# First weights as four tiles by half the rows, and block 1's layernorm root and scale moved into block 0's output stage

## The chip, the cores and the metric

The program runs on one core of one Trainium2 chip. The metric is the device time of one execution in microseconds (us), as a median over runs. A profiled execution also has a span, from its first to its last instruction; the span is about 1.4 us shorter than the time of the same run.

The engines are PE (TensorE, matmuls), PEld (its weight loads), DVE (VectorE), ACT (ScalarE), POOL (GpSimd) and SP (SyncE, which only issues DMAs here).

## The reference

Two layers read the same layernormed input of 2048 rows by 1024 features, in bf16, and their outputs are added to it.

```python
xn = layernorm(x)                                # 2048 x 1024, eps 1e-5
# A: diagonal state space layer, 1024 complex states
Bu = xn @ B_bar.T                                # complex
h[t] = Lam_bar * h[t-1] + Bu[t]                  # sequential over 2048 rows
yA = 2 * real(h @ C.T) + xn * Dskip
# B: dense, mish, dense, F = 3584
hB = xn @ w1 + b1
yB = (hB * tanh(softplus(hB))) @ w2
out = x + yA + yB
```

## The kernel before

The rows are worked in NB = 4 blocks of 512. A block has three stages on PE:

1. First product: `xn @ w1`, 28 tiles f of 128 columns, 8 matmuls each. DVE adds the bias and empties the PSUM bank into `hb`, ACT makes the mish in four groups of seven tiles.
2. Projection: `xn @ B`, 8 steps j with two PSUM banks each. DVE multiplies both banks with a table (`mt`), which turns the complex scan into a real one.
3. Output stage: `act @ w2` and `h @ C` into all 8 banks, while DVE does the scans.

Weights go through a ring of seven slots of 512 KB. Each helper call records one instruction with the buffers it reads and writes; semaphore waits follow from these. The order of calls is the order on each engine.

```python
    def ring_load():                                  # next weight item into its slot
        ...
        if kind == "w1":                              # all 1024 rows, 256 columns: runs of 512 B
            dst = ring[:, s, :].rearrange("p (k f) -> p k f", k=NK)
            src = B_w1[:, g * 256:(g + 1) * 256].rearrange("(k p) f -> p k f", p=P)
        else: ...                                     # w2
        SP.dma(lambda e: e.dma_start(dst, src), s_ring[s], writes=[b_ring[s]])
```

Block 1's layernorm is done during block 0. The statistics come at tiles 14 to 20, and then, all on DVE, the reciprocal root (15 small operations, a bit trick with three Newton steps) and four scalings:

```python
    def ln_rsqrt():
        ...                                           # v + eps, shift, subtract from the magic number
        for _ in range(3):                            # four operations a step
            ...
    def ln_scale(blk, q):
        vop(lambda e: e.tensor_scalar(xn[:, q, :], xx[:, i, q, :], mv[:, q, 0:1], rv[1][:, q:q + 1],
                                      op0=ALU.subtract, op1=ALU.mult), ...)

    def project_in(blk):
        for j in range(NJ):
            bank = banks_of(j)                        # 2 * ((j + 2) % 4)
            ...                                       # 16 matmuls into banks bank, bank + 1
            for s in range(2):                        # the table multiply: reads both banks
                vop(lambda e, ...: e.tensor_tensor(mt[:, s, :, :], u, tab..., op=ALU.mult), ...)
            ...                                       # an add and a subtract into hT

        def side(f):                                  # block 0: extra work after tile f
            if f == 13: ...                           # tables on ACT
            if f in (7, 8, 9, 10):
                coefficients(f - 7)
            if f in (9, 11, 12, 13):
                ln_skip(0, (9, 11, 12, 13).index(f))  # x += xn * Dskip
            if f in (14, 16, 18, 20):
                ln_stats_only(1, (f - 14) // 2)
            if f == 22:
                ln_rsqrt()
            if f in (23, 24, 25, 26):
                ln_scale(1, f - 23)
            ...                                       # transposes of B and C

        for f in range(NF):
            first_tile(blk, f)
            side(f)
        project_in(blk)
        ...
        for j in range(NJ):
            recur(blk, j)                             # scan of step j
            if blk == 0 and j == 0:
                mish_mul(3)
            if blk == 0:
                scale_C(j)
        ...
        tail(blk)                                     # output stage
```

## Time and profile before

| | before |
|---|---|
| time, median of 6 runs | 622.90 us (622.65 to 624.14) |
| span of the profiled run | 622.1 us |
| PE's share of the chain that ended last | 97% |
| PE's waits after its warm-up | 0.51 us for a weight load, 0.94 us for DVE |
| output stage of block 0 / of block 1, in the chain | 77.09 / 75.97 us |

A busy share does not bound a kernel; the chain does. PE has 97% of the chain, and one 512-column matmul costs 48.35 us / 224 = 215.9 ns in every block. The list of waits shows whom PE waited for, with the total, the number of times and the longest:

```profile
PE ps L465 <- POOL kon L333: 1.4, 1, 1.4
PE ps L727 <- DVE mt L674: 0.9, 1, 0.9
PE ps L504 <- DMA ring<-in_B_w_dram: 0.5, 1, 0.5
```

The first is the start of a warm-up. The other two are all that can be won by waiting less. The chain in order of time (start, length, what) shows where the second lies:

```profile
19.74 39.71 PE ps L649 x184
59.45 27.63 PE ps L669 x128
87.08 4.12 PE ps L727 x19
91.20 0.03 issue
91.22 2.37 DVE mt L674 x2
93.59 0.04 issue
93.63 70.54 PE ps L727 x326
164.17 48.35 PE ps L649 x224
```

At 87.08 us PE begins the output stage of block 0. Its 27th matmul needs bank 2, which DVE's last table multiply, from 91.22 us, has yet to read.

Why is DVE late? Its timeline (start, length, engine, line, operation, tiles, shapes, count; a bracket at the end is idle time before it) in the stretch before:

```profile
57.48 1.41 DVE L656 TENSOR_SCALAR hb<-ps,par 128x512 bf16<-128x512 f32 x2
58.81 0.16 DVE L415 TENSOR_SCALAR rv<-mv 128x4 f32<-128x4 f32 x1
...
63.05 0.16 DVE L425 TENSOR_TENSOR rv<-rv 128x4 f32<-128x4 f32 x1
63.13 0.74 DVE L656 TENSOR_SCALAR hb<-ps,par 128x512 bf16<-128x512 f32 x1
63.79 0.54 DVE L429 TENSOR_SCALAR xn<-xx,mv,rv 128x1024 bf16<-128x1024 bf16 x1
...
67.59 0.75 DVE L656 TENSOR_SCALAR hb<-ps,par 128x512 bf16<-128x512 f32 x1
68.25 2.35 DVE L674 TENSOR_TENSOR mt<-ps,tab 128x1024 bf16<-128x1024 f32 x2
70.64 0.42 DVE L677 TENSOR_TENSOR hT<-mt 128x512 bf16<-128x512 bf16 x1
70.98 0.41 DVE L679 TENSOR_TENSOR hT<-mt 128x512 bf16<-128x512 bf16 x1
71.53 2.35 DVE L674 TENSOR_TENSOR mt<-ps,tab 128x1024 bf16<-128x1024 f32 x2
```

There is no bracket: DVE never idles. The root (L415 to L425) and the scalings (L429) stand ahead of the table multiplies, the first of which starts at 68.25 us, although PE had finished its banks at about 59.45 + 27.63 / 8 = 62.9 us. One step takes DVE 71.53 - 68.25 = 3.28 us and PE 27.63 / 8 = 3.45 us, so eight steps win back only 1.4 us of the 5.35 us.

### The profile page before, as it was taken

How to read it: one execution, taken by the hardware profiler on the slowest of the kernel's cores; microseconds unless marked ns; L12 is line 12 of the kernel's file. 1: busy time of each engine (PE TensorE's matmuls, PEld its weight loads, DVE VectorE, ACT ScalarE, POOL GpSimd, SP SyncE). 2: the span in 40 equal slices, each digit the busy share in tenths (PEclk: the TensorE clock that was granted, in tenths of full speed). 3: DMA queues.
4: the chain of work that ended last, by engine and by line, in shares of the span. 5: the costliest groups of instructions: out<-in, count | busy, mean ns of one | idle time of the engine just before them, and what ended most of it. 6: DMA issues, size and time to landing. Idle time of an engine off the chain costs nothing.

```text
span 622.1 us, 7394 instructions
## 1 busy us (share of the span) xinstructions
PE 617.1 (99%) x2961; PEld 287.8 (46%) x2961; DVE 467.2 (75%) x690; ACT 244.6 (39%) x158; POOL 50.9 (8%) x47
## 2 busy tenths in 40 slices
PE   8999999999999999999999999999999999999998
PEld 7544444444444444444444444444444444444444
DVE  6799999999557599999047759999624856999603
ACT  5679996332069950000008992000000999000000
POOL 1999000000100000000010000000000000000000
DMA  8999996750265400784064430285304542033001
GB/s 246 246 245 263 236 170 190 187 165 0 101 209 164 135 2 9 232 172 129 14 189 143 162 101 1 71 223 158 90 35 135 151 154 67 1 117 120 1 0 68
DMA packets 124477, 79.41 MB, mean 128 GB/s; under 512 B 48923, under 2 KB 106907, under 8 KB 124443
## 3 DMA queue, kind: packets, MB, share of 16 engines
q1 hardware_dynamic: 120944, 71.64, 43.5%
q10 hardware_dynamic: 2538, 4.14, 1.8%
q0 software_dynamic: 960, 3.15, 1.7%
q8 instruction: 24, 0.39, 0.3%
q14 instruction: 11, 0.08, 0.0%
HBM read 63.19 MB, written 4.19 MB: 108 GB/s over the span
## 4 chain that ended last, share of the span: by engine, by line
PE 97%; DMA 1%; DVE 0%; SPq 0%; issue 0%
PE ps L727 48%; PE ps L649 30%; PE ps L669 18%; DMA ring<-in_B_w_dram 1%; PE ps L504 1%; DVE mt L674 0%; SPq L287 0%; PE ps L741 0%; PE ps L386 0%; SPq L291 0%; SPq L318 0%; DVE xx L795 0%
## 5 line engine op out<-in xcount | busy, mean ns | idle before, releaser
L727 PE MATMUL ps<-ring,act 128*128 128x512 bf16 x896 | 194.2, 379 | 0.9 <-DVE mt L674 0.9
L649 PE MATMUL ps<-xnT,ring 128*128 128x512 bf16 x856 | 185.4, 379 | 0.0
L627 ACT ACTIVATE act<-hb 128x3584 bf16<-128x3584 bf16 x16 | 50.9, 3183 | 246.3 <-DVE hb L656 246.0
L727 PEld LDWEIGHTS ps<-ring,act 128*128 128x128 bf16 x896 | 87.6, 98 | 106.9 <-DVE mt L674 1.4
L649 PEld LDWEIGHTS ps<-xnT,ring 128*128 128x128 bf16 x856 | 83.7, 98 | 100.8
L656 DVE TENSOR_SCALAR hb<-ps,par 128x512 bf16<-128x512 f32 x112 | 82.8, 747 | 56.5 <-PE ps L649 55.3
L669 PE MATMUL ps<-xnT,BT 128*128 128x512 bf16 x512 | 111.2, 379 | 0.0
L727 PE MATMUL ps<-CT,hT 128*128 128x512 bf16 x506 | 109.9, 379 | 0.0
L674 DVE TENSOR_TENSOR mt<-ps,tab 128x1024 bf16<-128x1024 f32 x64 | 75.3, 1219 | 13.3 <-PE ps L669 11.8
L669 PEld LDWEIGHTS ps<-xnT,BT 128*128 128x128 bf16 x512 | 50.1, 98 | 60.4
L727 PEld LDWEIGHTS ps<-CT,hT 128*128 128x128 bf16 x506 | 49.5, 98 | 59.7
L692 DVE TENSOR_TENSOR_SCAN hT<-cs,qi,hT 128x512 bf16<-128x512 f32 x48 | 58.9, 1267 | 0.0
L772 DVE TENSOR_TENSOR xx<-ps,xx 128x1024 bf16<-128x1024 f32 (+1 forms) x16 | 18.8, 1189 | 45.5 <-PE ps L727 45.4
L629 ACT ACTIVATE act<-act 128x3584 bf16<-128x3584 bf16 x16 | 51.0, 3190 | 0.2
L628 ACT ACTIVATE act<-act 128x3584 bf16<-128x3584 bf16 x16 | 51.0, 3190 | 0.2
L697 DVE TENSOR_TENSOR mt<-hT,tab 128x1024 bf16<-128x1024 bf16 x64 | 41.4, 688 | 1.1
L634 DVE TENSOR_TENSOR act<-act,hb 128x3584 bf16<-128x3584 bf16 x16 | 32.5, 2034 | 1.3 <-ACT act L629 1.3
L287 POOL DMA_DIRECT2D xx<-in_A_x_dram x12 | 6.7, 560 | 254.0 <-DVE xx L772 146.4
L603 ACT ACTIVATE ct<-CT,cs 128x512 f32<-128x512 bf16 x16 | 11.5, 718 | 28.8 <-DVE CT L605 24.5
L628 ACT ACT_TABLE_LOAD x16 | 20.5, 1283 | 0.3
L629 ACT ACT_TABLE_LOAD x16 | 20.5, 1283 | 0.3
L692 DVE TENSOR_TENSOR_SCAN hT<-cs,hT 128x512 bf16<-128x512 f32 x16 | 18.7, 1208 | 0.0
(82 smaller groups left out, 280.1 us busy)
## 6 DMA issues: line engine op xcount, KB each, us to landing
ring<-in_B_w_dram SPq DMA_DIRECT2D x112, 512.0 KB, 3.9
out_dram<-xx ACTq DMA_DIRECT2D x15, 256.0 KB, 2.1
xx<-in_A_x_dram POOLq DMA_DIRECT2D x12, 256.0 KB, 5.6
xx<-in_A_x_dram SPq DMA_DIRECT2D x3, 256.0 KB, 6.3
xx<-in_A_x_dram SPq DMA_DIRECT2D x2, 128.0 KB, 2.2
dsk<-in_A_Dskip_dram SPq DMA_DIRECT2D x1, 256.0 KB, 5.5
xnT<-xn SPq DMA_TRANSPOSE x12, 4.5
BT<-in_A_B_re_dram SPq DMA_TRANSPOSE x8, 5.7
```

Of the source, the lines that this page charges most:

```text
L627: aop(lambda e: e.activation(a, hs, AF.Exp), reads=[b_hb[g % 2]], writes=[b_act[g]])
L628: aop(lambda e: e.activation(a, a, AF.Ln, bias=1.0), reads=[b_act[g]], writes=[b_act[g]])
L629: aop(lambda e: e.activation(a, a, AF.Tanh), reads=[b_act[g]], writes=[b_act[g]])
L634: vop(lambda e: e.tensor_tensor(a, a, hs, op=ALU.mult), reads=[b_act[g], b_hb[g % 2]], writes=[b_act[g]])
L649: PE.mm(lambda e, k=k: e.matmul(ps[:, bank, :], lhsT=wt[:, k, fi * P:(fi + 1) * P], rhs=xnT[:, k, :], start=k == 0, stop=k == NK - 1), rea ...
L656: vop(lambda e: e.tensor_scalar(hb[:, hs, :], ps[:, bank, :], b1(f), None, op0=ALU.add), reads=[b_ps[bank], b_par], writes=[b_hbf[hs]])
L669: PE.mm(lambda e, j=j, ci=ci, k=k, bank=bank: e.matmul(ps[:, bank + ci, :], lhsT=BT[:, ci, j, k, :], rhs=xnT[:, k, :], start=k == 0, stop= ...
L674: vop(lambda e, s=s, u=u, j=j: e.tensor_tensor(mt[:, s, :, :], u, tab[:, s, j, :].unsqueeze(1).to_broadcast([P, 2, TB]), op=ALU.mult), rea ...
L692: vop(lambda e, ci=ci, init=init: e.tensor_tensor_scan(out=hT[:, ci, j, :], data0=cj("r", j).to_broadcast([P, TB]), data1=hT[:, ci, j, :], ...
L697: vop(lambda e, s=s: e.tensor_tensor(mt[:, s, :, :], hT[:, :, j, :], tab[:, s, j, :].unsqueeze(1).to_broadcast([P, 2, TB]), op=ALU.mult), ...
L727: PE.mm(lambda e: e.matmul(ps[:, u, :], lhsT=lhsT, rhs=rhs, start=st_, stop=last), reads=reads, writes=[b_ps[u]], first=st_, last=last)
L772: vop(lambda e: e.tensor_tensor(xr, src, xr, op=ALU.add), reads=b_ps[bank:bank + n] + [b_x], writes=[b_x])
```

## The change

It has three parts. *Weights:* the `w1` items become tiles of 512 rows by 512 columns, four of which hold the first eight tiles f; the contiguous runs are 1 KB instead of 512 B, the first tiles' matmuls are ordered to use the first load fully before the second, and slots are released in pairs. *Root and scale:* block 1's reciprocal root becomes one Sqrt on ACT and one reciprocal on DVE, and it and the four scalings move behind the first scan of the output stage; the transposes that use them come two tiles later. *Skip:* coefficients and skip stand one or two tiles sooner. The intent is to have weights sooner at the start and DVE on time for the projection.

```diff
         if kind == "w1":
-            dst = ring[:, s, :].rearrange("p (k f) -> p k f", k=NK)
-            src = B_w1[:, g * 256:(g + 1) * 256].rearrange("(k p) f -> p k f", p=P)
+            dst = ring[:, s, :].rearrange("p (k f) -> p k f", k=NK // 2)
+            r0 = (g % 2) * D // 2
+            src = B_w1[r0:r0 + D // 2, (g // 2) * 512:(g // 2 + 1) * 512].rearrange("(k p) f -> p k f", p=P)
...
+    def ln_root():
+        y = rv[1][:, :]
+        aop(lambda e: e.activation(y, mv[:, :, 1], AF.Sqrt, bias=kon[:, 2:3]), reads=b_mv + [b_kon], writes=[b_rv[1]])
+        vop(lambda e: e.reciprocal(y, y), reads=[b_rv[1]], writes=[b_rv[1]])
...
-    for f in range(NSPLIT):
+    for f in range(4):
         first_half(f, 0, 0, NK // 2)
-        if f == 3:
-            first_transpose(2)
-            first_copy(2, VE)
+    for f in range(4):
         first_half(f, 0, NK // 2, NK)
-        if f == 3:
-            first_transpose(3)
-            first_copy(3, VE)
+        if f in (1, 3):
+            q = 2 + f // 2
+            first_transpose(q)
+            first_copy(q, VE)
+    for f in range(4, NSPLIT):
+        first_half(f, 0)
...
-        if fi == 1:
+        if f % 4 == 3:
+            item_done()
             item_done()
...
-            if blk + 1 < NB and f in (7, 9, 11, 13):
-                transpose_dma((f - 7) // 2)
+            if blk + 1 < NB and f in (9, 11, 13, 15):
+                transpose_dma((f - 9) // 2)
...
-            if f in (7, 8, 9, 10):
-                coefficients(f - 7)
-            if f in (9, 11, 12, 13):
-                ln_skip(0, (9, 11, 12, 13).index(f))
+            if f in (5, 6, 7, 8):
+                coefficients(f - 5)
+            if f in (8, 9, 11, 12):
+                ln_skip(0, (8, 9, 11, 12).index(f))
             if f in (14, 16, 18, 20):
                 ln_stats_only(1, (f - 14) // 2)
-            if f == 22:
-                ln_rsqrt()
-            if f in (23, 24, 25, 26):
-                ln_scale(1, f - 23)
...
             if blk == 0 and j == 0:
                 mish_mul(3)
+                ln_root()
+                for q in range(NQ):
+                    ln_scale(1, q)
```

Cut: the indexing of the new tiles in the matmuls.

More of the change, by code (lines that the diff above doesn't have):

```diff
@@ L497, in build_kernel, with w1_tile @@
     NSPLIT = 5
+    def w1_tile(base, f, k):
+        s = (base + 2 * (f // 4) + k // (NK // 2)) % NRING
+        wt = ring[:, s, :].rearrange("p (k f) -> p k f", k=NK // 2)
+        return s, wt[:, k % (NK // 2), (f % 4) * P:(f % 4 + 1) * P]
     def first_half(f, half, k0=0, k1=NK):
-        s, fi = f // 2, f % 2
-        wt = ring[:, s, :].rearrange("p (k f) -> p k f", k=NK)
         ts = slice(half * 256, half * 256 + 256)
         for k in range(k0, k1):
-            PE.mm(lambda e, k=k: e.matmul(ps[:, f, ts], lhsT=wt[:, k, fi * P:(fi + 1) * P], rhs=xnT[:, k, ts],
-                                          start=k == 0, stop=k == NK - 1),
+            s, w = w1_tile(0, f, k)
+            PE.mm(lambda e, k=k, w=w: e.matmul(ps[:, f, ts], lhsT=w, rhs=xnT[:, k, ts],
+                                               start=k == 0, stop=k == NK - 1),
                   reads=[b_ring[s]] + [b.parts[k // 4] for b in b_xnT[2 * half:2 * half + 2]], writes=[b_ps[f]],
                   first=half == 0 and k == 0, last=half == 1 and k == NK - 1)
-    for f in range(NSPLIT):
+    for f in range(4):
         first_half(f, 0, 0, NK // 2)
-        if f == 3:
-            first_transpose(2)
-            first_copy(2, VE)
+    for f in range(4):
         first_half(f, 0, NK // 2, NK)
-        if f == 3:
-            first_transpose(3)
-            first_copy(3, VE)
+        if f in (1, 3):
[4 more added lines that the diff above has]
+        first_half(f, 0)
     aop(lambda e: e.activation(c("dt"), ldt, AF.Exp), reads=[b_par], writes=[b_cs["dt"]])
@@ L642, in first_tile @@
     def first_tile(blk, f):
-        s = n_item[0] % NRING
-        fi, bank, hs = f % 2, f % 8, f % (2 * GF)
-        wt = ring[:, s, :].rearrange("p (k f) -> p k f", k=NK)
+        bank, hs = f % 8, f % (2 * GF)
         if blk == 0 and f < NSPLIT:
@@ L648, in first_tile @@
         for k in range(0 if blk == 0 and f < NSPLIT else NK):
-            PE.mm(lambda e, k=k: e.matmul(ps[:, bank, :], lhsT=wt[:, k, fi * P:(fi + 1) * P], rhs=xnT[:, k, :],
-                                          start=k == 0, stop=k == NK - 1),
+            s, w = w1_tile(n_item[0], f % 4, k)
+            PE.mm(lambda e, k=k, w=w: e.matmul(ps[:, bank, :], lhsT=w, rhs=xnT[:, k, :],
+                                               start=k == 0, stop=k == NK - 1),
                   reads=[b_ring[s]] + b_xnT, writes=[b_ps[bank]], first=k == 0, last=k == NK - 1)
-        if fi == 1:
+        if f % 4 == 3:
+            item_done()
             item_done()
```

## The prediction

> **What bounds the kernel.** TensorE: the chain of waits gives PE 97% of the 622.1 us span. A 512-column matmul costs 215.9 ns (chain: 48.35 us for 224) in every stage, at granted clock 1.00, so only idle PE time can be won. The list of PE's waits has two holes after the warm-up: 0.51 us at 11.09 us, where the third tile of the first product waits for the second weight load (issued 3.78, landed 11.55 by the trace's DMA records); and 0.94 us at 92.69 us, where block 0's output stage needs a PSUM bank that VectorE has not read (releaser: mt, the table multiply).
>
> **What the change does.**
>
> 1. Weight loads. Same bytes and count, but contiguous runs of 1 KB instead of 512 B. In the DMA records the early 512 B packets took 28–32 ns, the 2 KB ones about 95; interpolated, an estimate of 50–55 ns for 1 KB, 10% less than two halves. (The Trainium skill, "DMA: Bandwidth & Descriptors", section "Why small descriptors are slow", gives a fixed overhead per packet; these times agree in direction.) Loads landed 1.6 us apart; I expect 1.45–1.5, so the second lands near 11.1 us. The first load still feeds 16 matmuls, so the 0.51 us hole shrinks to 0–0.2. Tile 4 now needs load 3 (landed 14.81 before) at about 14.4 us: a hole up to 0.3 us is possible. Net gain 0.3 us (0 to 0.5).
>
> 2. VectorE before block 0's projection. In the timeline the reciprocal root took 58.81 to 63.13 us and the four scalings 0.46 us each beyond the evictions: 6.2 us. VectorE began the table multiplies at 68.25 us although the first banks were complete at about 62.9, and recovers only 0.17 us a step (3.28 against PE's 3.45). Without the 6.2 us it reaches them on time and ends near 89.5 us, 3 us before PE needs the bank. The 0.94 us hole vanishes.
>
> 3. The work put back: one Sqrt on ScalarE, one reciprocal, four scalings after the first scan. ScalarE pays one more table switch, 1.28 us in this trace (the figure of the skill's "ScalarE: Activation LUTs", section "What ACT_TABLE_LOAD costs"), inside idle gaps of 4.3 us. VectorE finished that stage at 157.2 us with slack to 160.6, and starts it 4 us earlier: no cost. Later transposes of block 1 still end long before use. Coefficients and skip sooner fill VectorE's idle gaps at 20–29 us: no effect on PE.
>
> 4. Ring slots are released in pairs. Only load 13 is doubtful: it queues behind another pair of B transposes, lands at an estimated 50.5–52 us instead of 48.65, and is needed at 52.7. Probably no hole; about 1 us at worst.
>
> **Sum.** 0.94 + 0.3 = 1.25 us off the critical path, of the 6.2 us that VectorE sheds. Prediction 621.5 us against 622.8, range 620.5 to 623.0. Chances: faster by over 2% 0.5%, within 2% 99%, slower by over 2% 0.5%.
>
> **What would show it.** No wait of PE for DVE mt near 92 us; PE's wait for ring at 11 us at most 0.2 us; VectorE's first table multiply at about 63 us, thereafter waiting for PE; 1 KB packets in place of 512 B; one or two more ScalarE table loads; PE enters the 512-column matmuls at 19.3–19.5 us instead of 19.7.
>
> **What would make it wrong.** A new PE wait for ring at tile 4 (about 14.4 us) or near 52 us (load 13) that eats the gain; 1 KB packets not faster; run-to-run spread (1.5 us among the three runs before) as large as the gain.

## More of the kernel before

In the experiments the profiled run is one of the timed runs.

Block 1's x is loaded by the POOL queue, between two groups of GpSimd work that compute phases for the tables (`if j == 3: load_x(PO, 1, q)`).

## The result

| | before | after |
|---|---|---|
| time, median of 6 runs | 622.90 us (622.65 to 624.14) | 621.84 us (621.43 to 622.33) |
| span of the profiled run | 622.1 us | 620.9 us |
| PE enters the 512-column matmuls, in the chain | 19.74 us | 19.64 us |
| output stage of block 0, in the chain | 77.09 us | 75.97 us |
| last table multiply of block 0 ends | 93.58 us | 89.38 us |

The ratio of the fast runs is 0.998, with a 95% interval of 0.9967 to 0.9993. A ratio here is the mean time of one kernel's fast runs over that of the other's of the same rounds, so it is not quite the ratio of the medians. The gain of about 1.06 us is small but clear of the spread.

In the changed kernel the lines have other numbers: L661 is the first product, L682 the projection, L740 the output stage, L687 the table multiply, L388 the transposes of the first x tiles, L516 the first product's split tiles. PE's waits:

```profile
PE ps L472 <- POOL kon L335: 1.4, 1, 1.4
PE ps L388 <- DVE xn L376: 0.6, 1, 0.6
```

Both old waits are gone; a new one of 0.6 us stands in the start, at 7.86 us (see below). The chain over the same stretch has no DVE piece:

```profile
19.64 39.71 PE ps L661 x184
59.36 27.63 PE ps L682 x128
86.99 75.97 PE ps L740 x352
162.96 48.35 PE ps L661 x224
```

And DVE's timeline ahead of the projection:

```profile
53.76 3.38 DVE L669 TENSOR_SCALAR hb<-ps,par 128x512 bf16<-128x512 f32 x5
57.67 0.75 DVE L669 TENSOR_SCALAR hb<-ps,par 128x512 bf16<-128x512 f32 x1 [0.52 <-PE ps L661]
59.40 0.75 DVE L669 TENSOR_SCALAR hb<-ps,par 128x512 bf16<-128x512 f32 x1 [0.97 <-PE ps L661]
62.85 2.36 DVE L687 TENSOR_TENSOR mt<-ps,tab 128x1024 bf16<-128x1024 f32 x2 [2.70 <-PE ps L682]
...
66.30 2.36 DVE L687 TENSOR_TENSOR mt<-ps,tab 128x1024 bf16<-128x1024 f32 x2 [0.30 <-PE ps L682]
```

Now DVE waits for PE: 2.70 us before the first table multiply, and 0.30 us before each later one. Of the 1.2 us between the two profiled spans, 77.09 - 75.97 = 1.12 us come from the output stage and 19.74 - 19.64 = 0.1 us from the start.

### The profile page after: what moved, and what is told of

It reads as the page before. It is cut to its first block, busy times and chain, and to the rows that moved or that the text cites. A ratio compares the mean times of both kernels' runs of the same rounds, so it can differ in the third digit from the quotient of the medians.

```text
span 620.9 us, 7382 instructions
## 1 busy us (share of the span) xinstructions
PE 616.8 (99%) x2961; PEld 287.4 (46%) x2961; DVE 462.3 (74%) x676; ACT 247.9 (40%) x161; POOL 50.7 (8%) x47
## 4 chain that ended last, share of the span: by engine, by line
PE 98%; DVE 1%; DMA 1%; SPq 0%; issue 0%
PE ps L740 49%; PE ps L661 30%; PE ps L682 18%; PE ps L516 1%; DMA xx<-in_A_x_dram 1%; DVE stats L348 0%; PE ps L754 0%; DVE xn L376 0%; PE ps L388 0%; SPq L291 0%; DVE xnT L401 0%; DVE xx L808 0%; DVE mv L353 0%; DVE par L495 0%; DVE rs L372 0%
## 5 line engine op out<-in xcount | busy, mean ns | idle before, releaser
L740 PE MATMUL ps<-ring,act 128*128 128x512 bf16 x896 | 194.0, 379 | 0.0
L661 PE MATMUL ps<-xnT,ring 128*128 128x512 bf16 x856 | 185.4, 379 | 0.0
L740 PEld LDWEIGHTS ps<-ring,act 128*128 128x128 bf16 x896 | 87.7, 98 | 105.7
L661 PEld LDWEIGHTS ps<-xnT,ring 128*128 128x128 bf16 x856 | 83.7, 98 | 100.8
L682 PE MATMUL ps<-xnT,BT 128*128 128x512 bf16 x512 | 111.2, 379 | 0.0
L740 PE MATMUL ps<-CT,hT 128*128 128x512 bf16 x506 | 109.9, 379 | 0.0
L687 DVE TENSOR_TENSOR mt<-ps,tab 128x1024 bf16<-128x1024 f32 x64 | 75.4, 1220 | 17.2 <-PE ps L682 16.6
L682 PEld LDWEIGHTS ps<-xnT,BT 128*128 128x128 bf16 x512 | 50.1, 98 | 60.4
L740 PEld LDWEIGHTS ps<-CT,hT 128*128 128x128 bf16 x506 | 49.5, 98 | 59.7
```

The source lines that it names most:

```text
L661: PE.mm(lambda e, k=k, w=w: e.matmul(ps[:, bank, :], lhsT=w, rhs=xnT[:, k, :], start=k == 0, stop=k == NK - 1), reads=[b_ring[s]] + b_xnT, ...
L682: PE.mm(lambda e, j=j, ci=ci, k=k, bank=bank: e.matmul(ps[:, bank + ci, :], lhsT=BT[:, ci, j, k, :], rhs=xnT[:, k, :], start=k == 0, stop= ...
L687: vop(lambda e, s=s, u=u, j=j: e.tensor_tensor(mt[:, s, :, :], u, tab[:, s, j, :].unsqueeze(1).to_broadcast([P, 2, TB]), op=ALU.mult), rea ...
L740: PE.mm(lambda e: e.matmul(ps[:, u, :], lhsT=lhsT, rhs=rhs, start=st_, stop=last), reads=reads, writes=[b_ps[u]], first=st_, last=last)
```

## The experiments

The three parts can be taken alone, as they touch separate lines. All kernels gave a correct result. Each had five timed runs (half_packets six), beside runs of the kernel before on the same chip; no single gain of 1 us is 2%, so all verdicts are "same" and the intervals and the traces decide.

| kernel | weights | root and scale | skip | runs, us | ratio (95% interval) | PE waits for mt |
|---|---|---|---|---|---|---|
| ln_only | old | moved | old | 621.51 to 621.97 | 0.9981 (0.9968 to 0.9993) | none |
| skip_only | old | old | sooner | 621.95, 622.00, 622.93, 623.06, 623.07 | 0.9994 (0.9982 to 1.0007) | none in the profile |
| weights_only | new | old | old | 622.43 to 623.13 | 0.9998 (0.9984 to 1.0011) | 0.9 us |
| after_again | new | moved | sooner | 621.50 to 622.52 | 0.9985 (0.9972 to 0.9997) | none |
| undo_ln | new | old | sooner | 621.53 to 622.47 | 0.9977 (0.9965 to 0.9990) | none |
| no_weights | old | moved | sooner | 621.41 to 622.41 | 0.9980 (0.9968 to 0.9992) | none |

New weights with the moved root and scale and the old skip were not run.

### ln_only: the root and scale alone

The edit is the hunks with `ln_root`, the removed `ln_rsqrt` and `ln_scale` lines and the later transposes, on the kernel before.

> The kernel before with only the layernorm root and scale moved into the output stage. Theory (VectorE's backlog before the projection of block 0 is what makes PE wait at 92.7 us, and the root and scale are that backlog): PE's wait for DVE mt disappears, VectorE's first table multiply starts at 62.9 to 63.5 us instead of 68.25, the block 0 output stage takes 75.97 us in the chain instead of 77.09; span 621.0 us, 1.1 below the 622.1 before, time ratio 0.998. Rival A (the weight loads give the gain): no change, 622.1. Rival B (the sooner coefficients and skip are needed): the wait stays in part.

Measured: 621.79 us median, ratio 0.9981. The first table multiply starts at 62.37 us, and PE has no wait left but its warm-up. This part alone gives the whole gain, so rivals A and B fall as far as they say that another part is needed. PE's waits:

```profile
PE ps L470 <- POOL kon L333: 1.4, 1, 1.4
```

### skip_only and skip_again: the coefficients and skip alone

```diff
-            if f in (7, 8, 9, 10):
-                coefficients(f - 7)
-            if f in (9, 11, 12, 13):
-                ln_skip(0, (9, 11, 12, 13).index(f))
+            if f in (5, 6, 7, 8):
+                coefficients(f - 5)
+            if f in (8, 9, 11, 12):
+                ln_skip(0, (8, 9, 11, 12).index(f))
```

> The kernel before with only the coefficients and the skip sooner. The theory as predicted says that they give PE nothing: span 622.1 and the 0.94 us wait stays. But in the changed kernel VectorE evicted tile 13 at 38.1 us instead of 39.9, so rival B says that this alone puts VectorE about 1.8 us ahead, which is more than the 0.94 us that PE waits: first table multiply near 66.4 us, last one ends near 91.8 us, and the wait disappears too, span 621.0. Then the two parts are each sufficient and their gains do not add.

Measured: the profile shows what rival B said (first table multiply at 66.48 us, the last ends at 91.81 us, no wait of PE for mt, span 620.6 us), but three of five times were 622.93 to 623.07 us, as slow as the kernel before, and two near 622. In this profile DVE has a wait that the kernel before has not (DVE's waits from 20 to 62 us):

```profile
DVE hb L656 <- PE ps L649: 1.6, 2, 1.0
DVE stats L408 <- DMA xx<-in_A_x_dram: 0.7, 1, 0.7
```

DVE now comes so early to the statistics of block 1 that its x has not landed. That gave theory C: the landing of block 1's x decides what the sooner skip is worth. The kernel was run again for its scatter:

> skip_only once more, for its scatter. Theory C (the landing of block 1's x tile decides): times again either near 622.0 or near 623.0; if the profile falls on a slow one, VectorE's wait for x before the statistics is longer than 0.8 us, the last table multiply ends after PE wants the bank, and PE waits for mt. In skip_only the margin was 0.3 to 0.5 us (last multiply ended at 91.81, PE used the bank from 92.2).

Measured: 621.55, 621.89, 622.11, 622.14 and 624.12 us (ratio 0.9981, interval 0.9968 to 0.9994); the profile fell on the 624.12. In it, over the same 20 to 62 us, DVE's waits are

```profile
DVE stats L408 <- DMA xx<-in_A_x_dram: 5.3, 2, 3.8
DVE hb L656 <- PE ps L649: 1.6, 2, 1.0
```

and PE's, over the whole span, are

```profile
PE ps L465 <- POOL kon L333: 1.4, 1, 1.4
PE ps L727 <- DVE mt L674: 1.2, 1, 1.2
PE ps L669 <- DVE hb L656: 0.8, 1, 0.8
PE ps L386 <- DVE xn L374: 0.4, 1, 0.4
```

The four x loads, issued from 35.6 us on, landed at 42.1, 48.9, 49.7 and 50.2 us, against 42.0 to 45.5 in skip_only. DVE lost 5.3 us at the statistics and the hole came back, with a second one at the projection. Theory C holds on the trace of a slow run and the trace of a fast run of the same kernel. No profile fell on one of skip_only's runs near 623 us, so for these it is inferred.

### skip_x_early and skip_x_late: x sooner and later

skip_only with the POOL queue's x loads in another place:

```diff
     for j in range(NJ):
         phases(j)
-        if j == 3:
+        if j == 1:        # skip_x_early;  j == 4 in skip_x_late
             for q in range(NQ):
                 load_x(PO, 1, q)
```

> skip_only with block 1's x loads issued two phase groups earlier on the pool queue (about 26 instead of 36 us). Theory C: x has landed before VectorE asks for it, the statistics do not wait, first table multiply near 65.8 us, no wait of PE for mt; all five times near 621.9 (spans 620.3 to 620.8) instead of the scatter 621.95 to 623.07. Rival (the scatter has another cause, such as the narrow margin of under 1 us at the last bank, or the start): still two groups of times 1 us apart.

Measured: issued at 25.1 us, x landed from 31.3 to 36.6 us; DVE does not wait for it, the first table multiply starts at 65.33 us, PE has no wait for mt, and all five times lie between 621.44 and 622.37 us (ratio 0.9978, interval 0.9965 to 0.9990). The scatter is gone. So the sooner skip alone is enough, if x is there.

> skip_only with block 1's x loads one phase group later (about 41 instead of 36 us). Theory C: x lands near 46 us, VectorE waits for it about 4 to 5 us at the statistics, PE waits for mt about 3.5 to 4.5 us, all times near 626. Rival (x's landing is not what scatters skip_only): no change against skip_only, 622 to 623.

Measured: the direction is as theory C says, the size is not. x landed from 46.7 us on and DVE waited 5.3 us for it, as expected; all five times (622.90 to 624.45 us, median 623.55) are slower than skip_only's fast ones. But PE waited for mt only 1.2 us, and the times are near 623.5, not 626. The first table multiply came at 68.24 us, 1.8 us later than skip_only's 66.48, although the statistics were 4.8 us later (55.27 against 50.52 us for the last). DVE had won 3 us back: the 15 operations of the root took 2.9 us here (60.26 to 63.20 us) and 4.9 us in skip_only (55.49 to 60.39 us), and the first scaling 0.54 us against 1.58 us. In skip_only they ran while GpSimd was still at work (until 62.3 us), here GpSimd had ended at 59.95 us. A few operations are stretched, not all; of skip_only's:

```profile
56.12 1.12 DVE L418 TENSOR_SCALAR rv<-rv 128x4 int32<-128x4 int32 x1
57.27 0.16 DVE L421 TENSOR_TENSOR rv<-rv 128x4 f32<-128x4 f32 x1
57.47 0.55 DVE L422 TENSOR_TENSOR rv<-rv 128x4 f32<-128x4 f32 x1
```

The Trainium skill, "SBUF — State Buffer", section "SBUF: two separate sides", says that VectorE, in some kinds of operation, and GpSimd share a port pair that one of them holds for a whole instruction while the other fully blocks. This trace agrees only in part: the 1.12 us operation ended at 57.24 us, within 0.03 us of the end of a GpSimd operation (55.94 to 57.21 us), but the 0.55 us one ended at 58.02 us, inside the next one (57.32 to 58.89 us), and others took their usual 0.16 us beside it. So that GpSimd stretches them is not shown here beyond the coincidence in time. That part of my expectation was an error of mine: I took every DVE operation to cost the same whenever it ran.

### weights_only: the weight tiles alone

> The kernel before with only the weight tiles by half the rows and the first product's new order. Theory: 1 KB packets at 47 to 52 ns, loads land 1.5 us apart, the 0.51 us hole at 11 us is gone, but PE reaches the 512-column matmuls only 0.1 to 0.4 us sooner, because the second x tile's landing and the layernorm of the third and fourth x tile bound the start; the wait for DVE mt stays (about 0.9 us in the list, 1.1 in the chain). Span 621.7 to 622.0. Rival A: this part gives all, span 620.9. What also is asked: does the second x tile land at 5.5 us as in the changed kernel, or at 4.8 as before (then its delay there was chance).

Measured: 622.69 us median, ratio 0.9998. PE's waits still hold the one for mt:

```profile
PE ps L472 <- POOL kon L335: 1.4, 1, 1.4
PE ps L740 <- DVE mt L687: 0.9, 1, 0.9
```

The 1 KB packets are faster as predicted. From 9.0 to 12.5 us the DMAs moved 366 GB/s here and 294 GB/s in skip_only, whose loads are the old ones; the seven other traces with the old loads lie between 287 and 296, the four others with 1 KB between 352 and 358. A packet took on average 48 to 51 ns against about 33 ns for half of it. But PE gets nothing. The second x tile landed at 4.57 us, so its 5.50 us in the first profile of the changed kernel was chance, and with it the 0.6 us wait there. (A wait of this kind, 0.3 to 0.6 us, also stands in skip_again, skip_x_early, skip_x_late, no_weights and half_packets, with old loads and with new tiles.) And the 0.51 us wait for the second weight load was chance too: of eight traces with the old weight loads (the kernel before, ln_only, both of skip_only, both with x moved, extra_before, no_weights), only the first has it. From the first matmul on weights to the first 512-column matmul PE took 10.02 to 10.24 us in the other seven, and 10.02 to 10.24 us in the five traces with the change's weight loads.

### after_again: the whole change once more

> The whole change once more, on the same chip as the parts. Theory: span 620.9 again, ratio 0.998; if its second x tile lands near 4.8 us this time instead of 5.5, PE begins at 9.2 us instead of 9.46 and the span is 620.6.

Measured: 621.93 us median, ratio 0.9985, span 620.4 us. The second x tile landed at 4.84 us, PE's first matmul on weights began at 8.90 us instead of 9.46, and the wait in the start is gone.

### undo_ln and no_weights: the whole change less one part

> The changed kernel with the layernorm root and scale put back before the projection (so: weight tiles and sooner skip only). In skip_only the profile had no wait for mt (span 620.6) but three of five times were as slow as before; the profile shows VectorE waiting 0.7 us for block 1's first x tile, which landed at 41.95 us there, at 43.96 in the kernel before, at 39.1 to 40.4 with the 1 KB weight loads. Theory C: that landing decides whether the sooner skip is worth anything, and the faster weight loads bring it forward. Then here no wait of VectorE for x, no wait of PE for mt, all five times near 621.9, ratio 0.9985: the root and scale were not needed in the presence of the other two parts. Rival: only the root and scale give a stable gain, and this runs as before, 622.8, or scatters between the two as skip_only did.

Measured: 621.83 us median, ratio 0.9977, five times within 0.94 us, no wait of DVE for x, none of PE for mt; the first table multiply starts at 65.25 us. x landed at 39.1 us first and DVE asked for it at 40.75 us. So with the new weights and the sooner skip, the root and scale are not needed. The rival falls on this trace; five runs alone would be few. Four of the ten runs of skip_only and skip_again were slow, so five fast ones in a row would come by chance about once in 13 (0.6 to the fifth power, an estimate), here and in skip_x_early alike.

> The changed kernel without its weight part: root and scale moved, coefficients and skip sooner, the old weight loads. Theory: the root and scale alone give VectorE enough margin that a late x costs nothing; no wait for mt, times near 621.9, ratio 0.998, like the whole change. If the weight part brought the start forward, this is 0.2 us slower than the whole change by the trace (512-column matmuls from 19.3 instead of 19.1 us), which the times cannot resolve.

Measured: 621.78 us median, ratio 0.9980, no wait for mt, first table multiply at 62.92 us. So with the root and scale moved, the weights are not needed.

### half_packets: small packets in the new tiles

undo_ln with every weight load issued as two of half the size, so that `w1` runs are 512 B again:

```diff
...
-        SP.dma(lambda e: e.dma_start(dst, src), s_ring[s], writes=[b_ring[s]])
+        for c in range(2):
+            if kind == "w1":
+                d_, s_ = dst[:, :, c * 256:(c + 1) * 256], src[:, :, c * 256:(c + 1) * 256]
+            else:
+                d_, s_ = dst[:, c:c + 1, :], src[:, c:c + 1, :]
+            SP.dma(lambda e, d_=d_, s_=s_: e.dma_start(d_, s_), s_ring[s], writes=[b_ring[s]])
```

Cut: the ring's semaphores, which now count two loads each.

> undo_ln (weight tiles by half the rows and sooner skip, root and scale in the old place) with each weight load issued as two of half the size, so that the packets of the first weights are 512 B again while tiles, order and releases in pairs stay. If the packet size is what brings block 1's x forward (39 to 40 us in five traces with 1 KB, 41.5 to 44 in four with 512 B), x lands at 41.5 or later, VectorE waits for it, and times scatter between 622 and 623 like skip_only. If the release in pairs (fewer loads queued ahead of x) is what does it, x lands at 39 to 40 and the times stay at 621.9.

Measured: x landed at 42.6, 48.3, 49.0 and 49.9 us, DVE waited 3.9 us for it, and the times are 621.93 to 624.66 us (ratio 1.0008, interval 0.9995 to 1.0021). So the release in pairs alone does not bring x forward, and the times scatter again. That the packet size does is not shown. This kernel also issues twice as many loads, and it issues them later: loads 11 and 12 from 34.4 to 36.0 us, right ahead of x at 36.3 us, where undo_ln issued them at 30.1 and 31.0 us. For the rate at the start the packets are the likelier cause: 294 GB/s from 9.0 to 12.5 us, as with the old loads. Nor do these times show what a late x costs: in the profiled run PE has no wait for mt. The run showed something that I had not expected of it, in PE's waits:

```profile
PE ps L666 <- DMA ring<-in_B_w_dram: 2.3, 1, 2.3
PE ps L477 <- POOL kon L340: 1.4, 1, 1.4
PE ps L393 <- DVE xn L381: 0.5, 1, 0.5
```

PE waited from 53.1 to 55.44 us for load 13, whose second half was issued only at 51.38 us, behind two B transposes issued at 42.25 and 49.41 us, and landed at 55.39 us. That is the hole of the prediction's step 4, and all that the profiled run lost: 623.2 - 2.3 is 620.9 us, the span of the changed kernel. In the changed kernel load 13 landed at 46.29 us, over 6 us ahead of the moment at which PE asked for it here.

### extra_before and extra_after: useless work ahead of the projection

Six multiplies on DVE, of no use, after tile 26 of block 0, in the kernel before and in the changed one:

```diff
+            if f == 26:
+                for n in range(6):
+                    m = mt[:, n % 2, :, :].rearrange("p a t -> p (a t)")
+                    vop(lambda e, m=m: e.tensor_tensor(m, dsk[:], dsk[:], op=ALU.mult),
+                        reads=[b_dsk], writes=[b_m[n % 2]])
```

> The kernel before with six useless VectorE multiplies (0.6 us each, about 3.7 us) after tile 26 of block 0, ahead of the projection. Theory: VectorE's backlog is on the critical path there, so the last table multiply ends 3.7 us later, PE's waits for mt grow from 0.9 to about 4.6 us, time 622.8 + 3.7 = 626.5, ratio 1.006. Rival (the backlog only coincides with the wait): time grows by under 1 us.

Measured: 627.00 us median against 623.07 us in the same rounds, 3.9 us more, ratio 1.0061 (1.0048 to 1.0075). The six took 3.69 us, and PE's waits for DVE grew to 3.2 us for mt and 0.4 us at the projection, with another 0.4 us put down to "issue" there:

```profile
PE ps L727 <- DVE mt L674: 3.2, 2, 2.0
PE ps L465 <- POOL kon L333: 1.4, 1, 1.4
PE ps L669 <- DVE hb L656: 0.4, 1, 0.4
PE ps L669 <- issue: 0.4, 1, 0.4
```

DVE's work before the projection is on the critical path, about one for one (the interval means 3.0 to 4.7 us).

> The same six multiplies in the changed kernel. VectorE idles about 4.2 us before its first table multiply there (0.5 + 1.0 + 2.7) and has about 3 us more before PE needs the last bank, so 3.7 us cost nothing: no wait for mt, ratio to before 0.9985 as for the changed kernel. Rival: if VectorE's work as such bounds the kernel, it costs 3.7 us here too.

Measured: 621.95 us median, ratio 0.9977, no wait for mt. The six even took 5.18 us there, with GpSimd at work beside them until 61.99 us, and cost nothing: the last table multiply still ended at 89.04 us.

## Why the prediction was right, and where it was not

The predicted 621.5 us lay 0.3 us below the measured 621.84, in the range. That range, 620.5 to 623.0 us, also holds the time before, 622.90 us, so it could not by itself tell this gain from none. And it is luck that the 1.22 us between the two first spans met the sum of 0.94 + 0.3: the first term was 0.18 us too small, the second 0.2 us too large.

**Bound: right.** PE bounds the kernel, and only its idle time could be won. DVE shed 6.2 us before the projection; PE gained 1.1.

**Step 2 (DVE before the projection), "The 0.94 us hole vanishes": right, and shown to be the cause.** ln_only gives the whole gain; extra_before gives 3.9 us back for 3.7 us of work; extra_after gives nothing back. The first table multiply came at 62.85 us (said: about 63) and the last ended at 89.38 us (said: near 89.5). In the chain the hole was worth 1.12 us rather than 0.94.

**Step 1 (weight loads), "Net gain 0.3 us (0 to 0.5)": the term that was mis-sized.** It measured 0.1 us between the two first profiles, and nothing that stands out of the spread in all traces together. Loads landed 1.5 us apart, as said (the second at 10.17 us, sooner than the 11.1 us said), but I had read the 0.51 us hole from one profile as a property of the kernel. Seven further traces with the same loads have no such hole. The profiled run was itself a slow one, 623.57 us against a median of 622.90. The prediction that PE enters the 512-column matmuls at 19.3 to 19.5 us instead of 19.7 missed by the chain (19.64). Its feared hole at tile 4 did not come: load 3 landed at 13.18 us.

**Step 3 (the work put back): right in what it costs, wrong in one sentence.** ACT has two table loads more (40 against 38), each 1.28 us, and PE notices nothing. The figure is that of the Trainium skill, "ScalarE: Activation LUTs", section "What ACT_TABLE_LOAD costs", for the load alone; the page adds about 1.38 us of drain to every switch, and this trace shows no idle time of that size beside a load (0.3 us in all ahead of 16 of them). DVE ended block 0's scans at 155.1 us instead of 157.2. But "Coefficients and skip sooner fill VectorE's idle gaps at 20–29 us: no effect on PE" was wrong. Filling idle gaps is just what puts DVE ahead: skip_x_early and undo_ln remove the hole with the root and scale in their old place. The three parts are not a sum; they overlap on one hole.

**Missed: the weights act on something else.** Their effect is not in the start but at 40 us. With the change's weight part the first quarter of block 1's x lands at 39.1 to 40.4 us (five traces) instead of 41.3 to 44.0 us (six traces with the old loads and the x loads in their place), ahead of DVE's asking for it in undo_ln (40.75 us). Whether the packet size or the order of the loads does that stays open (half_packets). In the whole change this stays unseen, because the moved root and scale leave DVE about 3 us to spare. (An estimate: the kernel before asked for bank 2 at 92.69 us, 5.61 us after the chain's 87.08; 86.99 + 5.61 is 92.60 us in the changed kernel, and the last table multiply ended at 89.38.)

**Step 4 (slots in pairs, load 13): right that no hole would come, wrong in the size.** It landed at 46.29 us, not 50.5 to 52, even sooner than before (48.65). With 512 B packets and doubled issues the hole did come, 2.3 us.

**Open.** The other changes of the start cannot be resolved: the moment of the first 512-column matmul scatters from 18.57 to 19.58 us with the old loads and from 18.66 to 19.48 us with the new ones. Why in the slow runs nearly nothing of block 1's x lands for some 6 us (42.1 to 48.9 in skip_again, 42.6 to 48.3 in half_packets) was not found; the transposes of B share the DMA engines then, and in both traces one that was issued within 0.4 us of the first x load (at 35.41 and 36.59 us) landed only at 50.24 and 49.81 us, but I ran no test of it.

## What to carry to other kernels

Where one engine is busy from end to end, add up its holes first: the work taken off another engine is worth no more than the hole that it causes, here 1.1 of 6.2 us, and several remedies for one hole do not add up. Read a hole of half a microsecond in more than one profile before you count on it. When a time falls into two groups, look for a wait that a fast profile shows short and a slow one shows long, then move its cause sooner and later, as was done here with the x loads.

## What the Trainium skill lacked or had wrong

- "DMA: Bandwidth & Descriptors", section "Specifications", puts the least transfer for line rate at 512 B. Here 512 B packets moved 287 to 296 GB/s and 1 KB packets 352 to 366 GB/s, in the same stretch of the start. The per-packet overhead of section "Why small descriptors are slow" fits in direction; the page has no rate for 512 B packets on this chip.
- "SBUF — State Buffer", section "SBUF: two separate sides", tells of the port pair that VectorE and GpSimd share, but gives no size of the loss in a running kernel: 15 small VectorE operations took 4.9 us beside GpSimd work and 2.9 us after it, six multiplies 5.18 us and 3.69 us (that the ports are the reason is not shown).
- No page that I read warns that one profile can hold a wait which the next ones have not: 0.51 us for a weight load in one of eight traces, 0.6 us for an x tile in one of two profiles of the changed kernel itself.
